# A fixed order on every engine after the first chunk, and value products and the next scores in one burst

## The chip, the cores and the metric

The kernel runs on one core of one Trainium2 chip. The metric is the device time of one execution in microseconds. Three executions of the kernel before took 731.03, 731.56 and 733.35 us; their median is 731.56 us. Lower is better.

## The reference

Attention over 8 batches, 8 heads, 576 tokens and head size 64, with two sparse masks, feeds a gated network that takes the largest of three products:

```python
mask_local = (rel >= 0) & (rel < stride)                 # stride 32, heads 0 to 3
mask_strided = (rel >= 0) & (pos[None, :] % stride == pos[:, None] % stride)   # heads 4 to 7
attn = softmax(where(mask, q @ k.T / 8, -1e9))
x = (attn @ v) as (4608 tokens, 512)
h = np.maximum(np.maximum(x @ w1, x @ w2), x @ w3)       # (4608, 768)
return h @ w_out                                         # (4608, 512)
```

## The kernel before, in words

**Units and chunks.** Attention is cut into 32 units, four for each batch; a unit is two heads. In a batch the two strided units come first, then the two local ones. The network works on nine chunks of 512 tokens, and chunk c can start when the units of batch c are done.

**A unit.** `scores(n)` multiplies queries with keys into the PSUM tile `s_ps` (64 or 36 small matmuls, each run twice by the engine because they are float32: 128 or 72 matmuls in the trace, line 266). VectorE adds the mask, takes the maximum and subtracts it (`less_maximum`, lines 287 to 290), ScalarE takes the exponential (line 294), and VectorE sums, inverts, multiplies and transposes into `pt` (`probabilities`, lines 302 to 307). `values(n)` multiplies `pt` with the values into `o_ps` (line 363: 64 matmuls in a strided unit; line 333: 84 in a local one). `leading` (ScalarE, line 391) and `rest` (VectorE, line 395) split the result into the two float32r parts `xh` and `xl` that the network reads.

**A chunk.** It has 22 pieces. Pieces 0 to 17 are `ff_in`, 12 matmuls of 512 columns each (line 410), with `ff_max` behind (line 421 on ScalarE or 423 on VectorE; every third time also line 426 on ScalarE and 427 on GpSimd). Pieces 18 to 21 are `ff_out`, 18 such matmuls (line 436), with a copy and a store (lines 441, 442). I call these matmuls dense. Their results go to two PSUM buffers `f_ps`, so piece i+2 waits until the result of piece i is read.

**What sets the order.** The opening (all weights, the units of batches 0 and 1, and chunk 0) is written out by hand in `OPENING`; each letter is a step, and `pin` holds it in program order. From batch 2 on, `pinned[0]` is False: a scheduler orders the instructions of all engines after its own estimate. The program there puts `begin(n)` (scores to transpose) ahead of pieces 0, 5, 10 and 15 and `end(n)` (values, leading, rest) ahead of pieces 4, 9, 14 and 19. Chunks 7 and 8 have no units beside them.

Of the kernel before, what the change touches and what calls it, by code (L numbers as in the profile page):

```python
# [15 lines left out]
B, H, S, D = 8, 8, 576, 64  # L16
STRIDE = 32
DM, DF, DO = 512, 768, 512
P = 128
# [12 lines left out]
MB = 5  # L32
MS = STRIDE // 4
PAIRED = 2
CH = 512
NCHUNK = B * S // CH
W_LEAST = 2.0**-15
W_MOST = 122877.984375
NKC = DM // P
NJ = DF // P  # L40
# [8 lines left out]
N5 V4 A10 A11 M3 F4 B9 C9 B10 F5 C10 H4 M4 A12 S6 M5 X6 A13 F6 B11 B12 F7 M6 C11 L4 F8 C12 B13 E6 M7 A14  # L49
C13 V5 A15 A16 F9 M8 B14 C14 B15 A17 B16 M9 C15 B17 A18 C16 A19 F10 M10 F11 C17 B18 F12 C18 M11 H5 M12  # L50
N6 F13 A20 F14 L5 A21 B19 V6 C19 A22 M13 F15 B20 C20 M14 F16 M15 A23 F17 B21 M16 B22 C21 C22 S7 M17 B23
X7 C23 H6 O0 E7 L6 N7 O1 Q0 O2 V7 Q1 H7 L7 O3 Q2 Q3
"""


# [1 line left out]
def fused_kernel(ctx, tc, qT, kT, qk_loc, qk_str, v_loc, v_str, m_loc, m_str, w1, w2, w3, w_out, out):  # L57
# [17 lines left out]
    early_ps = ExitStack()  # L75
    ps_e = early_ps.enter_context(tc.tile_pool(name="ps_e", bufs=1, space=bass.MemoryType.PSUM))

    pinned = [True]

    def pin(ins):  # L80

        return tc.keep_in_program_order(ins) if pinned[0] else ins


    mloc = const.tile([P, MB, TK], F32, name="mloc")
# [104 lines left out]
    units = [(b, p) for b in range(B) for p in (2, 3, 0, 1)]  # L190
    loaded = {}

    def load_qk(n):
        if n >= len(units):
            return
        b, p = units[n]
        t = (io_early if n in (2, 3) else io).tile([P, 2, S], F32, name="qk_t", bufs=2)
        if b < EARLY:
            pin(nc.sync.dma_start(out=t[:, 0, :], in_=qT[b, p]))
            pin(nc.sync.dma_start(out=t[:, 1, :], in_=kT[b, p]))  # L200
        else:
            src = qk_loc[b - EARLY, p, 0] if p < 2 else qk_str[b - EARLY, p - 2].rearrange("p x s -> p (x s)")
            src = src.rearrange("p (x h s) -> p x h s", x=2, h=2)
            for h in range(2):
                hs = slice(h * D, (h + 1) * D)
                pin(nc.sync.dma_start(out=t[hs], in_=src[hs, :, h, :]))
        loaded[n] = [t.rearrange("p x s -> p (x s)")]
# [27 lines left out]
    state = {}  # L235

    def scores(n):


        b, p = units[n]  # L240
        t = loaded[n][0]
        s_ps = s_places[0 if n in (0, 2) else 1]
        mask = mloc.rearrange("p m k -> p (m k)") if p < 2 else mstr.unsqueeze(1).broadcast_to([P, MS, NI])
        first = n < 8
        if first:
            for h in range(2):
                flat = s_ps[:, h, : MB * TK] if p < 2 else s_ps[:, h, : 32 * MS].rearrange("p (m k) -> p m k", m=MS)
                pin(nc.tensor.matmul(flat if p < 2 else flat[:, :, :NI], unit, mask, start=True, stop=False))  # L248
        nm, w, at = (MB, TK, TK) if p < 2 else (MS, NI, 32)
        pairs = p >= 2 and b >= PAIRED  # L250
        for m in range(nm):
            for j in range(4):
                if p < 2:
                    u = j * MB + m
                    if u >= NT:
                        continue

                    q0, k0 = 32 * u, S + 32 * u - 32
                else:

                    q0 = NI * (j * MS + m)
                    k0 = S + q0
                k1 = m * 64 + j % 2 * 32 if pairs else m * at
                for h in range(2):
                    hs = slice(h * D, (h + 1) * D)
                    pin(nc.tensor.matmul(  # L266
                        s_ps[32 * j : 32 * (j + 1), h, k1 : k1 + w],
                        t[hs, q0 : q0 + 32],
                        t[hs, k0 : k0 + w],
                        start=not first,  # L270
                        stop=not first or m == (2 if p < 2 and j == 3 else nm - 1),
                    ))
        if pairs:
            s = s_ps.rearrange("p h (m r k) -> p h m r k", r=2, k=32)[:, :, :, :, :NI]
            flat, mask, axes = s, mpair.unsqueeze(1).unsqueeze(1), AX.XY
            wide = lambda x: x[:, :, :nm].unsqueeze(3).unsqueeze(4).broadcast_to(list(s.shape))
        else:
            s = s_ps[:, :, : nm * at].rearrange("p h (m k) -> p h m k", m=nm)[:, :, :, :w]
            flat, mask, axes = (s_ps[:, :, : nm * w] if p < 2 else s), mask.unsqueeze(1), AX.X
            wide = lambda x: x[:, :, :nm].unsqueeze(3).broadcast_to([P, 2, nm, w])  # L280
        state[n] = s_ps, s, wide, nm, 2 * at if pairs else at, axes, None if first else (flat, mask)

    def less_maximum(n):
        s_ps, s, wide, nm, at, axes, masked = state[n]
        if masked:
            flat, mask = masked
            pin(nc.vector.tensor_tensor(out=flat, in0=flat, in1=mask.broadcast_to(list(flat.shape)), op=ALU.add))  # L287
        mx = att.tile([P, 2, MS], F32, name="mx")
        pin(nc.vector.tensor_reduce(out=mx[:, :, :nm], in_=s, op=ALU.max, axis=axes))
        pin(nc.vector.tensor_tensor(out=s, in0=s, in1=wide(mx), op=ALU.subtract))  # L290

    def exponentials(n):
        s = state[n][1]
        pin(nc.scalar.activation(out=s, in_=s, func=AF.Exp, scale=SCALE))  # L294

    def probabilities(n):

        s_ps, s, wide, nm, at, axes, _ = state[n]
        sm = att.tile([P, 2, MS], F32, name="sm")

        sums = sm[:, :, :nm] if nm * at == 512 else s_ps[:, :, 512 - MS : 512 - MS + nm]
        pin(nc.vector.tensor_reduce(out=sums, in_=s, op=ALU.add, axis=axes))
        pin(nc.vector.tensor_scalar(out=sums, in0=sums, scalar1=EPS, scalar2=None, op0=ALU.add))
        pin(nc.vector.reciprocal(out=sm[:, :, :nm], in_=sums))
        pin(nc.vector.tensor_tensor(out=s, in0=s, in1=wide(sm), op=ALU.mult))
        pt = att.tile([P, 2, 512], F32, name="pt")
        pin(nc.vector.transpose(pt[:, :, : nm * at], s_ps[:, :, : nm * at]))  # L307
        state[n] = pt
# [80 lines left out]
    def leading(n):  # L389
        for src, hi, lo in state[n]:  # L390
            pin(nc.scalar.copy(out=hi, in_=src))  # L391

    def rest(n):
        for src, hi, lo in state.pop(n):
            pin(nc.vector.tensor_tensor(out=lo, in0=src, in1=hi.bitcast(F32), op=ALU.subtract))  # L395
# [4 lines left out]
    def ff_in(c, j, i):  # L400
        if not ps_f:
            early_ps.close()
            ps_f.append(ctx.enter_context(tc.tile_pool(name="ps_f", bufs=2, space=bass.MemoryType.PSUM)))
        f_ps = ps_f[0].tile([P, 512], F32, name="f_ps")
        hi, lo = x_chunk(c)
        wh, wl = weight[i, j]

        for kc in (2, 3, 0, 1):
            for n, (w, x) in enumerate(((wh, hi), (wh, lo), (wl, hi))):
                pin(nc.tensor.matmul(  # L410
                    f_ps, w[:, kc, :], x[:, kc, :], start=(kc == 2 and n == 0), stop=(kc == 1 and n == 2)
                ))
        hs[c, j, i] = f_ps
# [15 lines left out]
    def ff_out(c, t):  # L429
        f_ps = ps_f[0].tile([P, 512], F32, name="f_ps")  # L430
        ts = slice(t * P, (t + 1) * P)
        for j in range(NJ):
            hh, hl = hs[c, j]
            wh, wl = weight[None, j]
            for n, (h, w) in enumerate(((hh, wh), (hl, wh), (hh, wl))):
                pin(nc.tensor.matmul(f_ps, h[:, ts], w, start=(j == 0 and n == 0), stop=(j == NJ - 1 and n == 2)))  # L436
        hs[c, "out", t] = f_ps

# [2 lines left out]
        pin(nc.scalar.copy(out=o_sb, in_=hs.pop((c, "out", t))))  # L441
        pin(nc.scalar.dma_start(out=out[c * CH + t * P : c * CH + (t + 1) * P, :], in_=o_sb))

    def chunk(c):
        def both(do, then, *args):
            do(c, *args)
            then(c, *args)

        pieces = [lambda j=j, i=i: both(ff_in, ff_max, j, i) for j in range(NJ) for i in range(3)]
        return pieces + [lambda t=t: both(ff_out, ff_store, t) for t in range(CH // P)]  # L450


    def begin(n):
        scores(n)
        load_qk(n + 2)
        less_maximum(n)
        exponentials(n)
        probabilities(n)

    def end(n):  # L460
        values(n)
        load_v(n + 2)
        leading(n)
        rest(n)

    load_weights(1, nc.scalar)
    pin(nc.scalar.activation(out=nothing, in_=nothing, func=AF.Exp))
# [5 lines left out]
    for n in (2, 3):  # L473
# [7 lines left out]
    load_v(5)  # L481
    load_weights(len(sources))
    steps = {
        "S": scores, "X": less_maximum, "E": exponentials, "N": probabilities, "V": values, "H": leading, "L": rest,
        "A": lambda n: convert_begin(), "B": lambda n: convert_bits(), "C": lambda n: convert_end(),
        "F": lambda n: ff_in(0, n // 3, n % 3), "M": lambda n: ff_max(0, n // 3, n % 3),
        "O": lambda n: ff_out(0, n), "Q": lambda n: ff_store(0, n),
# [1 line left out]
    for step in OPENING.split():  # L489
# [3 lines left out]
            load_qk(n + 2)  # L493
        if what == "V" and n >= 4:
            load_v(n + 2)
    pinned[0] = False

    for b in range(2, B):
        for i, piece in enumerate(chunk(b - 1)):
            if i % 5 == 0 and i < 20:  # L500
                begin(4 * b + i // 5)
            if i % 5 == 4:
                end(4 * b + i // 5)
            piece()
    for c in range(B - 1, NCHUNK):
        for piece in chunk(c):
            piece()


# [64 lines left out]
```

## Time and profile before

| | |
|---|---|
| median of three executions | 731.56 us |
| the profiled execution | 728.72 us |
| its span, first to last instruction | 727.0 us |
| TensorE busy (PE) | 694.8 us, 96% |
| weight loads (PEld) | 560.2 us, 77% |
| VectorE, ScalarE, GpSimd | 313.8, 171.1, 123.0 us |
| matmuls, weight loads | 8448 and 8448 |
| chain that ended last, TensorE's share | 86% |

Each matmul has one weight load ahead of it, which runs beside the matmul before. The chain that ended last is followed back from the last instruction, so a large share of one engine in it says that this engine's work sets the time. Matmul durations in the rows are longer than their spacing, because each starts while the one before drains; the spacing of the starts is what counts.

### The profile page before, as it was taken

The page shows a single profiled execution, that of the slowest core. Times are in us where ns is not written, and L with a number is a line of the kernel's source. Part 1 is how long each engine was busy: PE and PEld are TensorE (multiplying, and loading weights), DVE is VectorE, ACT ScalarE, POOL GpSimd, SP SyncE. Part 2 cuts the span into 40 slices and gives each one's busy share as a digit, 9 for nine tenths or more (in the row PEclk, how much of TensorE's full clock was granted, in tenths as well). Part 3 has the DMA queues.
Part 4 walks back from the last instruction along what each step waited for, and adds up shares of the span by engine and source line. Part 5 has one row for each costly group of instructions (what it writes and reads, how often), then busy time and mean ns, then how long its engine had stood idle before and what let it go on. Part 6 is the DMA issues. An engine that isn't in the chain of part 4 may idle for free.

```text
span 727.0 us, 18760 instructions
## 1 busy us (share of the span) xinstructions
PE 694.8 (96%) x8448; PEld 560.2 (77%) x8448; DVE 313.8 (43%) x527; ACT 171.1 (24%) x346; POOL 123.0 (17%) x129
## 2 busy tenths in 40 slices
PE   6369899999999999999999999999999999999997
PEld 5258677888788878888788878887888788888886
DVE  6778995445334442545155514552344401101110
ACT  2546663121211221221112211212122211111111
POOL 4337572011001110111001100110001101100110
PEclk9569999999999999999999999999999999999999
DMA  7998011322222123212221222232220010000001
GB/s 242 263 306 305 25 31 63 96 67 71 71 77 55 55 76 107 54 54 62 90 82 58 63 73 62 62 82 73 62 55 22 15 44 1 0 30 29 1 1 58
DMA packets 35808, 55.35 MB, mean 76 GB/s; under 512 B 5200, under 2 KB 18512, under 8 KB 35728
## 3 DMA queue, kind: packets, MB, share of 16 engines
q1 hardware_dynamic: 30016, 44.19, 21.0%
q10 hardware_dynamic: 5712, 9.96, 3.7%
q8 instruction: 66, 1.08, 0.6%
q14 instruction: 14, 0.11, 0.1%
HBM read 44.70 MB, written 9.44 MB: 74 GB/s over the span
## 4 chain that ended last, share of the span: by engine, by line
PE 86%; DVE 1%; ACT 0%; issue 0%; DVEq 0%
PE f_ps L410 57%; PE f_ps L436 21%; PE s_ps L266 4%; PE o_ps L333 2%; PE o_ps L363 2%; ACT work L441 0%; DVE work L163 0%; DVE h_max L423 0%; PE s_ps L248 0%; DVE o_ps L160 0%; DVE work L166 0%; DVEq L166 0%; DVEq L160 0%
## 5 line engine op out<-in xcount | busy, mean ns | idle before, releaser
L410 PE MATMUL f_ps<-xh,w 128*128 128x512 f32 x1296 | 415.3, 395 | 2.7 <-ACT h_max L421 1.9
L410 PEld LDWEIGHTS f_ps<-xh,w 128*128 128x128 f32 x1296 | 243.8, 188 | 56.8 <-ACT h_max L421 2.3
L410 PE MATMUL f_ps<-xl,w 128*128 128x512 f32 x648 | 253.3, 391 | 0.0
L427 POOL TENSOR_TENSOR hl<-h_max,hh 128x512 fp32r<-128x512 f32 x54 | 69.6, 1289 | 532.4 <-ACT hh L426 532.4
L423 DVE TENSOR_TENSOR h_max<-f_ps,h_max 128x512 f32<-128x512 f32 x108 | 74.6, 690 | 187.9 <-PE f_ps L410 187.8
L436 PE MATMUL f_ps<-wNone,hh 128*128 128x512 f32 x432 | 140.6, 396 | 0.4 <-ACT work L441 0.4
L410 PEld LDWEIGHTS f_ps<-xl,w 128*128 128x128 f32 x648 | 122.1, 188 | 24.0
L436 PEld LDWEIGHTS f_ps<-wNone,hh 128*128 128x128 f32 x432 | 81.0, 188 | 18.9 <-ACT work L441 1.3
L436 PE MATMUL f_ps<-wNone,hl 128*128 128x512 f32 x216 | 85.1, 394 | 0.0
L426 ACT CAST hh<-h_max 128x512 fp32r<-128x512 f32 x54 | 33.5, 620 | 200.8 <-DVE h_max L423 200.8
L395 DVE TENSOR_TENSOR xl<-o_ps,xh 128x320 fp32r<-128x320 f32 (+11 forms) x96 | 28.2, 349 | 84.1 <-ACT xh L391 84.1
L266 PEld LDWEIGHTS s_ps<-qk_t 64*32 64x32 f32 x3200 | 34.4, 110 | 22.8 <-issue 20.1
L441 ACT COPY work<-f_ps 128x512 f32<-128x512 f32 x36 | 21.0, 588 | 120.7 <-PE f_ps L436 120.7
L421 ACT COPY h_max<-f_ps 128x512 f32<-128x512 f32 x54 | 31.7, 586 | 74.1 <-PE f_ps L410 42.7
L266 PE MATMUL s_ps<-qk_t 64*32 64x18 f32 (+1 forms) x3200 | 39.6, 206 | 8.8 <-issue 6.3
L436 PEld LDWEIGHTS f_ps<-wNone,hl 128*128 128x128 f32 x216 | 40.6, 188 | 8.2
L294 ACT ACTIVATE s_ps<-s_ps 128x640 f32<-128x640 f32 (+2 forms) x32 | 20.3, 634 | 83.1 <-DVE s_ps L290 82.8
L287 DVE TENSOR_TENSOR s_ps<-s_ps,mpair 128x576 f32<-128x576 f32 x12 | 9.2, 767 | 68.1 <-PE s_ps L266 68.1
L391 ACT CAST xh<-o_ps 128x320 fp32r<-128x320 f32 (+11 forms) x96 | 24.3, 329 | 34.9 <-PE o_ps L333 30.4
L307 DVE STREAM_TRANSPOSE pt<-s_ps 128x640 f32<-128x640 f32 (+2 forms) x32 | 31.4, 980 | 0.7
L333 PEld LDWEIGHTS o_ps<-pt,v_t 32*64 32x64 f32 x1344 | 18.6, 141 | 16.2 <-issue 10.2
L333 PE MATMUL o_ps<-pt,v_t 32*64 32x64 f32 (+1 forms) x1344 | 22.3, 238 | 7.2 <-DVE xl L395 3.3
(49 smaller groups left out, 336.3 us busy)
## 6 DMA issues: line engine op xcount, KB each, us to landing
out<-work ACTq DMA_DIRECT2D x36, 256.0 KB
w<-in_w SPq DMA_DIRECT2D x17, 512.0 KB
qk_t<-in_qT SPq DMA_DIRECT2D x28, 288.0 KB
qk_t<-in_kT SPq DMA_DIRECT2D x28, 288.0 KB
v_t<-in_v_str SPq DMA_DIRECT2D x48, 128.0 KB
v_t<-in_v_loc SPq DMA_DIRECT2D x48, 96.0 KB
wNone<-in_w_out SPq DMA_DIRECT2D x6, 512.0 KB
v_t<-in_v_str SPq DMA_DIRECT2D x16, 72.0 KB
```

Of the source, the lines that this page charges most:

```text
L266: pin(nc.tensor.matmul(s_ps[32 * j : 32 * (j + 1), h, k1 : k1 + w], t[hs, q0 : q0 + 32], t[hs, k0 : k0 + w], start=not first, stop=not fir ...
L307: pin(nc.vector.transpose(pt[:, :, : nm * at], s_ps[:, :, : nm * at]))
L333: pin(nc.tensor.matmul(o[h * D : (h + 1) * D, j, 32 * max(m, 0) : 32 * max(m, 0) + width], v[js, h, m + 1, :], pt[js, h, m * TK + 32 : m * ...
L391: pin(nc.scalar.copy(out=hi, in_=src))
L395: pin(nc.vector.tensor_tensor(out=lo, in0=src, in1=hi.bitcast(F32), op=ALU.subtract))
L410: pin(nc.tensor.matmul(f_ps, w[:, kc, :], x[:, kc, :], start=(kc == 2 and n == 0), stop=(kc == 1 and n == 2)))
L421: pin(nc.scalar.copy(out=a, in_=f_ps))
L423: pin(nc.vector.tensor_tensor(out=a, in0=f_ps, in1=a, op=ALU.max))
L426: pin(nc.scalar.copy(out=hh, in_=a))
L427: pin(nc.gpsimd.tensor_tensor(out=hl, in0=a, in1=hh.bitcast(F32), op=ALU.subtract))
L436: pin(nc.tensor.matmul(f_ps, h[:, ts], w, start=(j == 0 and n == 0), stop=(j == NJ - 1 and n == 2)))
L441: pin(nc.scalar.copy(out=o_sb, in_=hs.pop((c, "out", t))))
```

## The change

From chunk 1 on the scheduler's freedom is gone: `pin` is now always `keep_in_program_order`, and a new loop writes out the order. The value products of unit n stand ahead of pieces 3, 8, 13 and 18 (`BURSTS`), and the scores of unit n+1 directly behind them; then come the split of unit n, the mask and maximum of n+1, the piece itself, the exponential, and one piece later the probabilities, with the transpose split off into `transposed` behind that piece's `ff_max`. The scores of unit 8 move into the opening, behind the values of unit 7. In `ff_out` the low weight part now comes ahead of the low half of h. The number of instructions that compute is the same.

```diff
+BURSTS = (3, 8, 13, 18)
-X7 C23 H6 O0 E7 L6 N7 O1 Q0 O2 V7 Q1 H7 L7 O3 Q2 Q3
+X7 C23 H6 O0 E7 L6 N7 O1 Q0 O2 V7 S8 Q1 H7 L7 O3 Q2 Q3
-    pinned = [True]
-    def pin(ins):
-        return tc.keep_in_program_order(ins) if pinned[0] else ins
+    pin = tc.keep_in_program_order
-            for n, (h, w) in enumerate(((hh, wh), (hl, wh), (hh, wl))):
+            for n, (h, w) in enumerate(((hh, wh), (hh, wl), (hl, wh))):
-    pinned[0] = False
-    for b in range(2, B):
-        for i, piece in enumerate(chunk(b - 1)):
-            if i % 5 == 0 and i < 20:
-                begin(4 * b + i // 5)
-            if i % 5 == 4:
-                end(4 * b + i // 5)
-            piece()
+    for c in range(1, NCHUNK):
+        coming = None
+        if c == 1:
+            coming = 8
+            less_maximum(coming)
+        for i in range(3 * NJ + CH // P):
+            if i in BURSTS and c < B - 1:
+                n = 4 * (c + 1) + BURSTS.index(i)
+                coming = n + 1 if n + 1 < len(units) else None
+                values(n)
+                if coming:
+                    scores(coming)
+                load_v(n + 2)
+                leading(n)
+                rest(n)
+                if coming:
+                    load_qk(coming + 2)
+                    less_maximum(coming)
+                since = i
+            elif i == 0:
+                since = 0
++            if i < 3 * NJ:
+                ff_in(c, i // 3, i % 3)
+            else:
+                ff_out(c, i - 3 * NJ)
+            if coming and i == since:
+                exponentials(coming)
+            if coming and i == since + 1:
+                probabilities(coming)
++            if i < 3 * NJ:
+                ff_max(c, i // 3, i % 3)
+            else:
+                ff_store(c, i - 3 * NJ)
+            if coming and i == since + 1:
+                transposed(coming)
+                coming = None
```

In the rows of the order below, a float32 matmul counts once (the trace shows it twice), and line numbers of after are two higher or lower (363 is 365, 266 is 264, 410 is 412, 436 is 438, 333 is 335, 395 is 397, 423 is 425).

TensorE in chunk 1, around the values of unit 8; `o_ps<-pt,v_t` are values, `s_ps<-qk_t` scores, `f_ps` dense. Before:

```order
L410 MATMUL f_ps<-xh,w_1_805 128x512
L363 MATMUL o_ps<-pt,v_t 64x2x18 x32
L410 MATMUL f_ps<-xh,w_1_815 128x512
L410 MATMUL f_ps<-xl,w_1_815 128x512
L410 MATMUL f_ps<-xh,w_1_815 128x512 x2
L410 MATMUL f_ps<-xl,w_1_815 128x512
L410 MATMUL f_ps<-xh,w_1_815 128x512 x2
L410 MATMUL f_ps<-xl,w_1_815 128x512
L410 MATMUL f_ps<-xh,w_1_815 128x512 x2
L410 MATMUL f_ps<-xl,w_1_815 128x512
L410 MATMUL f_ps<-xh,w_1_815 128x512
L266 MATMUL s_ps<-qk_t 32x18 x64
```

One piece of 12 dense matmuls stands between the values of unit 8 and the scores of unit 9. After:

```order
L412 MATMUL f_ps<-xl,w_0_663 128x512
L412 MATMUL f_ps<-xh,w_0_663 128x512
L365 MATMUL o_ps<-pt,v_t 64x2x18 x32
L264 MATMUL s_ps<-qk_t 32x18 x64
L412 MATMUL f_ps<-xh,w_1_805 128x512
L412 MATMUL f_ps<-xl,w_1_805 128x512
```

The two stand together, and the pieces between such bursts are five.

TensorE at the end of chunk 1, the values of unit 11. Before:

```order
L436 MATMUL f_ps<-wNone_1664,hh 128x512
L333 MATMUL o_ps<-pt,v_t 64x64 x7
L436 MATMUL f_ps<-wNone_1719,hh 128x512
L333 MATMUL o_ps<-pt,v_t 64x64 x4
L436 MATMUL f_ps<-wNone_1719,hl 128x512
L436 MATMUL f_ps<-wNone_1719,hh 128x512
L333 MATMUL o_ps<-pt,v_t 64x64 x3
L333 MATMUL o_ps<-pt,v_t 64x32 x8
L333 MATMUL o_ps<-pt,v_t 64x64 x14
L333 MATMUL o_ps<-pt,v_t 64x32 x6
L436 MATMUL f_ps<-wNone_1485,hh 128x512
```

The scheduler put dense matmuls into the middle of the values, so that they come in three parts. After:

```order
L412 MATMUL f_ps<-xh,w_5_1466 128x512
L335 MATMUL o_ps<-pt,v_t 64x64 x14
L335 MATMUL o_ps<-pt,v_t 64x32 x8
L335 MATMUL o_ps<-pt,v_t 64x64 x14
L335 MATMUL o_ps<-pt,v_t 64x32 x6
L264 MATMUL s_ps<-qk_t 32x18 x64
L438 MATMUL f_ps<-wNone_1485,hh 128x512 x2
```

They are whole, ahead of the first `ff_out`. The scores of units 12, 16, 20, 24 and 28, which before stand in two parts (2 and 62 matmuls), are whole too.

VectorE in chunk 1, from the split of unit 8 on. Before:

```order
L395 TENSOR_TENSOR xl<-o_ps,xh 128x384
L395 TENSOR_TENSOR xl<-o_ps,xh 128x192
L423 TENSOR_TENSOR h_max<-f_ps,h_max 128x512
L287 TENSOR_TENSOR s_ps<-s_ps,mpair 128x32x18
L289 TENSOR_REDUCE mx<-s_ps 128x16
L290 TENSOR_TENSOR s_ps<-s_ps,mx 128x32x18
L423 TENSOR_TENSOR h_max<-f_ps,h_max 128x512
L302 TENSOR_REDUCE sm<-s_ps 128x16
```

After:

```order
L397 TENSOR_TENSOR xl<-o_ps,xh 128x384
L397 TENSOR_TENSOR xl<-o_ps,xh 128x192
L285 TENSOR_TENSOR s_ps<-s_ps,mpair 128x32x18
L287 TENSOR_REDUCE mx<-s_ps 128x16
L288 TENSOR_TENSOR s_ps<-s_ps,mx 128x32x18
L299 TENSOR_REDUCE sm<-s_ps 128x16
L300 TENSOR_SCALAR sm<-sm 128x16
L301 RECIPROCAL sm<-sm 128x16
L302 TENSOR_TENSOR s_ps<-s_ps,sm 128x32x18
L425 TENSOR_TENSOR h_max<-f_ps,h_max 128x512
L309 STREAM_TRANSPOSE pt<-s_ps 128x1024
```

Between the split and the probabilities no `h_max` stands any more, and one now stands ahead of the transpose.

## Rows read from the trace of the kernel before

**Rows 1.** The page: granted TensorE clock in 40 slices (tenths); the queue of instruction packets.
```profile
PEclk9569999999999999999999999999999999999999
...
q8 instruction: 66, 1.08, 0.6%
```

**Rows 2.** Busy time in stretches: PE, PEld, DVE, ACT, POOL, each (xcount); then clock, DMA.
```profile
105.00:727.00 622.00, 617.80 (x6734) 498.59 (x6732) 229.86 (x387) 117.61 (x246) 69.70 (x55) 1.00 0.18 55
```

**Rows 3.** Waits of PE, 130 us to the end: who waited, total us, times, longest.
```profile
PE f_ps L436 <- ACT work L441: 0.4, 2, 0.2
```

**Rows 4.** Timeline of PE around values of unit 8, scores of unit 9: start, us, what.
```profile
141.99 0.39 PE L410 MATMUL f_ps<-xh,w 128*128 128x512 f32 x1
142.30 1.14 PE L363 MATMUL o_ps<-pt,v_t 64*64 64x36 f32 x64
143.37 0.50 PE L410 MATMUL f_ps<-xh,w 128*128 128x512 f32 x1
143.71 0.39 PE L410 MATMUL f_ps<-xl,w 128*128 128x512 f32 x1
143.94 0.63 PE L410 MATMUL f_ps<-xh,w 128*128 128x512 f32 x2
...
146.00 0.39 PE L410 MATMUL f_ps<-xh,w 128*128 128x512 f32 x1
146.32 1.42 PE L266 MATMUL s_ps<-qk_t 64*32 64x18 f32 x128
```

**Rows 5.** Timeline of PE, values of unit 11 at the end of chunk 1.
```profile
191.64 0.36 PE L333 MATMUL o_ps<-pt,v_t 32*64 32x64 f32 x14
...
192.37 0.34 PE L333 MATMUL o_ps<-pt,v_t 32*64 32x64 f32 x8
...
193.31 0.89 PE L333 MATMUL o_ps<-pt,v_t 32*64 32x64 f32 x62
```

**Rows 6.** Timeline of PE, the opening: scores with values directly behind.
```profile
14.27 1.12 PE L266 MATMUL s_ps<-qk_t 64*32 64x64 f32 x72
15.32 1.70 PE L374 MATMUL o_ps<-pt,v_t 18*64 18x18 f32 x128
```

**Rows 7.** Timeline of PEld, the opening: idle time ahead and its releaser in brackets.
```profile
11.14 0.55 PEld L266 LDWEIGHTS s_ps<-qk_t 64*32 64x32 f32 x42 [1.02 <-issue]
...
42.41 0.32 PEld L266 LDWEIGHTS s_ps<-qk_t 64*32 64x32 f32 x29 [4.47 <-issue]
```

**Rows 8.** Busy time in stretches that end where PEld stood still for "issue".
```profile
0.00:11.10 11.10, 5.23 (x222) 4.48 (x222) 4.27 (x10) 3.12 (x5) 7.49 (x28) 1.00 0.83 258
11.10:19.60 8.50, 7.39 (x254) 5.11 (x254) 7.78 (x15) 2.13 (x4) 0.96 (x2) 1.00 0.66 186
19.60:34.50 14.90, 4.15 (x255) 3.68 (x255) 11.89 (x21) 7.18 (x14) 5.26 (x6) 0.57 0.95 298
34.50:42.40 7.90, 3.09 (x127) 2.60 (x128) 3.24 (x7) 2.51 (x6) 1.87 (x2) 0.50 1.10 294
```

**Rows 9.** Busy time in two stretches with the same number of weight loads.
```profile
7.10:11.14 4.04, 3.13 (x160) 2.70 (x149) 2.43 (x7) 0.40 (x1) 1.93 (x8) 1.00 0.96 256
...
296.90:301.40 4.50, 4.50 (x159) 3.68 (x152) 1.51 (x3) 0.94 (x3) 0.00 (x0) 1.00 0.23 59
```

**Rows 10.** Busy time and clock in stretches with idle TensorE.
```profile
18.20:21.50 3.30, 1.31 (x73) 0.89 (x72) 2.44 (x4) 0.97 (x2) 1.89 (x2) 1.00 0.73 208
21.60:25.00 3.40, 0.00 (x0) 0.00 (x0) 1.38 (x2) 1.22 (x3) 0.61 (x1) 0.50 0.73 216
...
84.00:88.00 4.00, 2.15 (x10) 1.49 (x9) 3.66 (x6) 2.15 (x5) 2.54 (x3) 1.00 0.07 16
```

**Rows 11.** Timeline of PEld, dense matmuls while the clock is at half.
```profile
47.04 0.33 PEld L410 LDWEIGHTS f_ps<-xl,w 128*128 128x128 f32 x1
47.47 0.76 PEld L410 LDWEIGHTS f_ps<-xh,w 128*128 128x128 f32 x2
```

**Rows 12.** Timeline of DVE: mask (first) and transpose (last step) of unit 9.
```profile
147.79 0.77 DVE L287 TENSOR_TENSOR s_ps<-s_ps,mpair 128x576 f32<-128x576 f32 x1 [0.61 <-PE s_ps L266]
...
153.44 1.25 DVE L307 STREAM_TRANSPOSE pt<-s_ps 128x1024 f32<-128x1024 f32 x1
```

More of the change, by code (lines that the diff above doesn't have):

```diff
@@ L305, in probabilities, with transposed @@
         pin(nc.vector.tensor_tensor(out=s, in0=s, in1=wide(sm), op=ALU.mult))
+        state[n] = s_ps, nm, at
+    def transposed(n):
+        s_ps, nm, at = state[n]
         pt = att.tile([P, 2, 512], F32, name="pt")
@@ L442, in ff_store @@
         pin(nc.scalar.dma_start(out=out[c * CH + t * P : c * CH + (t + 1) * P, :], in_=o_sb))
[L444 to L464, printed above, removed]
     load_weights(1, nc.scalar)
@@ L483, in fused_kernel @@
     steps = {
-        "S": scores, "X": less_maximum, "E": exponentials, "N": probabilities, "V": values, "H": leading, "L": rest,
+        "S": scores, "X": less_maximum, "E": exponentials, "N": lambda n: (probabilities(n), transposed(n)),
+        "V": values, "H": leading, "L": rest,
         "A": lambda n: convert_begin(), "B": lambda n: convert_bits(), "C": lambda n: convert_end(),
@@ L495, in fused_kernel @@
             load_v(n + 2)
-    pinned[0] = False
-    for b in range(2, B):
-        for i, piece in enumerate(chunk(b - 1)):
-            if i % 5 == 0 and i < 20:
-                begin(4 * b + i // 5)
-            if i % 5 == 4:
-                end(4 * b + i // 5)
-            piece()
-    for c in range(B - 1, NCHUNK):
-        for piece in chunk(c):
-            piece()
+    for c in range(1, NCHUNK):
[19 more added lines that the diff above has]
+                since = 0
+            if i < 3 * NJ:
+                ff_in(c, i // 3, i % 3)
[5 more added lines that the diff above has]
+                probabilities(coming)
+            if i < 3 * NJ:
+                ff_max(c, i // 3, i % 3)
[4 more added lines that the diff above has]
+                coming = None
 _INS = ["qT", "kT", "qk_loc", "qk_str", "v_loc", "v_str", "m_loc", "m_str", "w1", "w2", "w3", "w_out"]
```

## The prediction

> **What bounds the kernel now.** I read the slices of the page first: the clock is low only in the first tenth, at full level from there on [rows 1]. Then the busy time by stretch: from 105 us to the end TensorE works 617.8 of 622.0 us [rows 2], and its waits on other engines there come to 0.4 us [rows 3]. VectorE works 229.9 and ScalarE 117.6 us of the same stretch [rows 2]; what they do is hidden as long as nobody waits. So a time can only change in TensorE's own spacing or by a new wait of TensorE. The opening is left as it was, but for the scores of unit 8.
>
> The spacing is in the timeline [rows 4]. Dense matmuls start every 0.227 us (143.71 to 143.94 is one step). Around a burst of small matmuls this is disturbed: the first small one starts 0.31 us after the last dense one (141.99 to 142.30); the last of the 64 starts about 143.22 (the group ends at 143.44, and one takes 0.22); 0.15 us later comes the first dense one at 143.37, and the next 0.34 us after that. Without a burst two dense steps would stand there, 0.45 us. So each burst pays 0.31 + 0.15 + 0.34 - 0.45 = 0.35 us for being a burst, whatever is in it.
>
> **The change, part by part.**
>
> *Fewer bursts.* Before, values and the next scores are two bursts with 12 dense matmuls between them; after, they are one, 24 times (units 7 and 8 to 30 and 31). Each saves 0.35 us and pays for the seam between the two kinds of small matmul. The trace has one seam, scores with values directly behind: the group of 72 begins at 14.27 and ends at 15.39, its last matmul starts about 15.17, the first value matmul at 15.32 [rows 6], so 0.15. In a group neighbours start about 0.015 apart (0.92 us over 63 steps [rows 4]), and the entry from dense costs 0.31. The seam lies between 0.015 and 0.31; I take 0.13, near the one that I see. 24 x (0.35 - 0.13) = 5.3 us; the bounds give 8.0 and 1.0.
>
> *No split bursts.* The values of units 11, 15, 19, 23, 27 and 31 come in three parts [rows 5], the scores of units 12, 16, 20, 24 and 28 in two. Whole, they save 6 x 2 + 5 = 17 bursts at 0.35, 6.0 us. With 0.4 us [rows 3], which come from two `ff_out` pieces that the scheduler let end together, that makes 6.4. The sum of gains is 5.3 + 6.4 = 11.7, about **12 us** with the small delays of later dense steps after each burst.
>
> *Instructions arrive in packets.* This is what speaks against the change. The page has a queue of 66 instruction packets [rows 1]; 16,896 matmuls and weight loads by 66 are 256 each, 128 pairs. In the opening the weight loads stand still four times for "issue", 1.0 to 4.5 us, the first and the last shown [rows 7]. Counted in loads these stops come after load 222, then 254, 255 and 128 further on [rows 8]: one packet is 128 loads, and a few semaphore instructions make up the missing ones. So TensorE stops at borders of packets, when the next has not come. From load 70 or so to the end of the first stop 149 loads took 4.04 us; elsewhere 152 loads in 4.50 us ran without a stop [rows 9]. I read from it: about 150 loads, one packet and what is read ahead, cannot go by in less than some 4.0 to 4.5 us.
>
> Before, this never bites in the later part: the 12 dense matmuls between values and scores take 2.7 us and give the packet its time. After, 150 loads fit into one burst: some 55 values at 0.0145 and 95 scores at 0.0097 (1.24 us for 128 [rows 4]) with the seam are 1.8 us, of a local unit 1.5; I take 1.7. A burst that holds such a stretch from end to end stops for 4.0 - 1.7 = 2.3 us. Which ones do follows from counting: from the last stop at load 859 every 128 loads (less the semaphores) through the new order of TensorE. The borders lie late in the scores of units 13, 20, 24 and 29, near matmul 99, 88, 123 and 114 of 128, with 150 loads of burst ahead; one lies just behind the scores of unit 17, 3.3 us after the packet was ordered, and stops about 0.7. 4 x 2.3 + 0.7 = **9.9 us**. With 4.5 us in place of 4.0 it is 4 x 2.8 + 1.2 = 12.4, with 3.8 it is 8.9. If the count is shifted against the borders, other bursts stop: over all shifts I count 8.9 to 15.7, mean 12.9.
>
> The Trainium skill says otherwise (Runtime: NRT & Kernel Launch, Instruction fetch mechanics): blocks of 256 instructions, but 2048 of them held for TensorE, and a crossing mostly hidden. Blocks of 256 agree with the 66 packets; 2048 held does not agree with a stop after 222 loads and 222 matmuls [rows 8]. By that page the stops would be 0 and the sum the first rival below.
>
> *The clock.* In the opening a stretch with two idle spells of TensorE (0.89 us of loads in 3.30) was followed by half the granted clock; 4.0 us with 1.49 us of loads, dense ones around the idle spell, kept the full one [rows 10]. A stop of 2.3 us inside 2 us of small matmuls lies between these. At half level dense matmuls start 0.43 us apart [rows 11] instead of 0.227, so 3 us of it (a stretch at half is 3.4 long [rows 10]) lose 3 x 0.47 = 1.4 us. I take one fall among the four long stops, **1.4 us**; none and all are in the rivals.
>
> *The other engines.* In the new order VectorE does the split, the mask and the maximum ahead of the piece's `h_max`. From mask to end of transpose a unit took 6.9 us, pieces between included (147.79 to 154.69 [rows 12]). After, the next values come five pieces, 13.6 us, behind the scores: 5 us and more are spare. The tightest is piece 3, whose first copy (ScalarE, line 421) now waits behind the exponential: some 6.9 us after the burst began, needed at 7.9 (values, scores, two pieces). So it costs nothing; without that microsecond TensorE would wait once a chunk, six times. The loads on SP's queue keep their place behind the burst that frees their buffer, two units ahead. The order in `ff_out` gives GpSimd 0.23 us more for the last low half, which nobody waits for [rows 3].
>
> **The sum.** -12.0 + 9.9 + 1.4 = -0.7 us. The profiled execution took 728.72 us, so 728.0; against the median of 731.56, which lies 2.8 above that execution, 730.9 us. About 0.3%, 2.2 us, is what a measurement of this kernel can tell from no change; the forecast is the same.
>
> **The rivals.**
>
> 1. *No stops.* If the stops of the opening belong to its start or its busy DMA, all 12 us remain: 719.6. For it: the DMA share there is 0.66 to 1.10 [rows 8] against 0.18 later [rows 2]. Against it: the even distance of the stops. 10%.
> 2. *Stops, but a cheap seam and a clock that holds:* seam 0.02 saves 2.6 more, no fall: -12.0 - 2.6 + 9.9 = -4.7, so 726.9. For it: weight loads of 32 columns may go in beside the last values. 23%.
> 3. *Other borders.* If my count is off, 13 to 15.7 us of stops: -12.0 + 13 (or 15.7) + 1.4 = +2.4 to +5.1, so 734 to 736.7. 10%.
> 4. *The clock falls at every stop.* Slower: five falls cost 7.0, -12.0 + 9.9 + 7.0 = +4.9, so 736.5. The place is the dense matmuls behind the scores of units 13, 17, 20, 24 and 29. It decides from the third fall on (-2.1 + 3 x 1.4 = +2.1). For it: the half clock after the idle spells of the opening [rows 10]. Against it: the values ahead of each stop keep TensorE busy. 15%.
> 5. *`f_ps` late at piece 3*, six waits of up to 1 us: +5 at most, 736. 2%.
>
> **How the numbers follow.** The forecast has 40%. Faster by over 0.3%: rivals 1 and 2 and the edge of the forecast, 0.35. Within: the rest of the forecast and the edge of rival 3, 0.40. Slower: rivals 3, 4 and 5, 0.25. The range holds the forecast, rival 2 with a seam still shorter stops could add to, and rivals 3 to 5 up to their far ends: 725.5 to 737.0. Left out are rival 1 and falls of the clock on top of other borders, some 2 in 10.
>
> **What would show it.** Right: in the profile after, TensorE or its loads idle for "issue" around 2.3 us late in the scores of units 13, 20, 24 and 29, about 25 bursts less than before, dense starts 0.227 apart elsewhere, and the clock at 1.00 but for a slice or two. Rival 1 shows no idle time over 0.4 us behind 105 us; rival 4 shows slices of 0.5 clock behind each stop; rival 5 shows TensorE waiting for line 423's counterpart on ScalarE. The forecast is wrong if the packets of instructions are not what stopped the opening, or if a seam costs as much as a fresh entry.

## The result and the profile after

The change makes the kernel slower by a third of a per cent: 732.65 us (median of 20 executions, 729.98 to 737.31) against 729.79 us for the kernel before in the same comparison (20 executions, 728.45 to 733.64). The ratio is 1.0034, with a 95% interval of 1.0018 to 1.0050; that is 1.3 to 3.6 us, 2.5 in the middle. The time lies inside the range of the prediction, but not in the forecast: "the same" was expected, by a gain of 0.7 us, and a small loss came. The mechanism comes nearest to rival 4: the clock fell behind four of the stops.

The profiled execution of after took 737.31 us, the longest of the 20, so its span says little by itself. The page of after, its span, busy times and granted clock in 40 slices (tenths), against [rows 1]:

```profile
span 735.6 us, 18767 instructions
...
PE 693.7 (94%) x8448; PEld 569.4 (77%) x8448; DVE 312.9 (43%) x527; ACT 171.3 (23%) x346; POOL 122.3 (17%) x129
...
PEclk9559999999999999999999999999999999999999
```

PE works 1.1 us less than before, 693.7 against 694.8, and yet the span is 8.6 us longer. Most of that is in the opening. I cut both traces at the first value product of unit 7, the last step ahead of the edit (124.57 us before, 130.77 after). Stretches of before and then of after: length, then busy us of PE, PEld, DVE, ACT and POOL with counts, granted clock, DMA share, GB/s.

```profile
0.00:124.50 124.50, 96.49 (x1866) 76.82 (x1866) 97.65 (x161) 60.03 (x114) 61.20 (x81) 0.89 0.59 180
124.57:727.00 602.43, 598.23 (x6583) 483.33 (x6582) 216.13 (x366) 111.11 (x232) 61.78 (x48) 1.00 0.18 55
```

```profile
0.00:130.70 130.70, 100.91 (x1866) 80.27 (x1866) 98.14 (x161) 60.25 (x114) 60.62 (x81) 0.86 0.55 172
130.77:735.60 604.83, 592.74 (x6583) 489.14 (x6582) 214.74 (x366) 111.01 (x232) 61.67 (x48) 0.99 0.18 54
```

The opening holds the same 1866 matmuls in both, and takes 6.2 us longer in this one execution of after, with a lower clock (0.86 against 0.89). It varies from execution to execution: in the nine experiments, eight of them with the same opening up to there, the values of unit 7 begin some 125 to 130 us into the span. So I compare kernels by the stretch from there to the end: 602.43 us before, 604.83 after, **+2.4 us**, which agrees with the medians. In that stretch PE is busy 5.5 us less, and idle 12.1 us (604.83 - 592.74) against 4.2. The idle time has one name. Waits of PEld from 130 us on, before and then after: who waited for what, us in total, times, longest.

```profile
PEld s_ps L266 <- issue: 9.5, 27, 0.4
PEld o_ps L333 <- issue: 7.9, 24, 0.4
PEld o_ps L363 <- issue: 4.2, 12, 0.4
```

```profile
PEld s_ps L264 <- issue: 8.6, 5, 2.3
PEld o_ps L335 <- issue: 4.6, 13, 0.4
PEld o_ps L365 <- issue: 4.2, 12, 0.4
PEld f_ps L412 <- issue: 0.7, 1, 0.7
```

Three things are to be seen. The many pauses of 0.4 us or less are entries from dense matmuls into small ones: 63 before, 25 after, so the bursts are merged and whole. Waits on another engine are gone (before had two on ScalarE). And there are five pauses of up to 2.3 us in the scores and one of 0.7 in the dense, which no row of before shows behind the opening.

**A merged burst.** Timeline of PE in after, values of unit 10 with scores of unit 11 behind them (start, us, what), against [rows 4]:

```profile
162.84 0.39 PE L412 MATMUL f_ps<-xh,w 128*128 128x512 f32 x1
163.16 1.14 PE L365 MATMUL o_ps<-pt,v_t 64*64 64x36 f32 x64
164.23 0.97 PE L264 MATMUL s_ps<-qk_t 64*32 64x64 f32 x72
165.13 0.50 PE L412 MATMUL f_ps<-xh,w 128*128 128x512 f32 x1
165.47 0.40 PE L412 MATMUL f_ps<-xl,w 128*128 128x512 f32 x1
```

The entry (162.84 to 163.16) and the two steps at the end are those of before. The last value matmul starts about 164.08, 0.22 us ahead of the group's end at 164.30, and the first score at 164.23: the seam is 0.15, and over the 24 merged bursts it is 0.147 (behind values of a local unit) or 0.153 (behind those of a strided one).

**The stops.** Timeline of PEld in after, units 9, 13, the dense behind 17, units 20, 24 and 29; in brackets the idle time ahead and what ended it:

```profile
146.69 0.63 PEld L264 LDWEIGHTS s_ps<-qk_t 64*32 64x32 f32 x64
148.68 0.63 PEld L264 LDWEIGHTS s_ps<-qk_t 64*32 64x32 f32 x64 [1.35 <-issue]
...
222.96 0.93 PEld L264 LDWEIGHTS s_ps<-qk_t 64*32 64x32 f32 x100
225.50 0.24 PEld L264 LDWEIGHTS s_ps<-qk_t 64*32 64x32 f32 x28 [1.61 <-issue]
...
304.40 0.19 PEld L412 LDWEIGHTS f_ps<-xl,w 128*128 128x128 f32 x1 [0.66 <-issue]
...
349.37 0.83 PEld L264 LDWEIGHTS s_ps<-qk_t 64*32 64x32 f32 x88
352.52 0.48 PEld L264 LDWEIGHTS s_ps<-qk_t 64*32 64x32 f32 x40 [2.31 <-issue]
...
428.13 1.27 PEld L264 LDWEIGHTS s_ps<-qk_t 64*32 64x32 f32 x124
431.13 0.14 PEld L264 LDWEIGHTS s_ps<-qk_t 64*32 64x32 f32 x4 [1.73 <-issue]
...
533.65 1.05 PEld L264 LDWEIGHTS s_ps<-qk_t 64*32 64x32 f32 x115
536.27 0.17 PEld L264 LDWEIGHTS s_ps<-qk_t 64*32 64x32 f32 x13 [1.57 <-issue]
```

The loads stand still behind load 100, 88, 124 and 115 of 128 in units 13, 20, 24 and 29, within one of the places that the counting gave, and once behind unit 17. The stop of unit 9, in the middle of its 128 loads, was not foreseen. As the distance from one start of a matmul to the next, less an ordinary step, the six cost 1.42 (unit 9), 1.70, 0.39, 2.38, 1.81 and 1.64 us, 9.3 together.

What the loads wait for can be read as well, because the trace records when each instruction packet of queue q8 was carried. The stretch of the stop of unit 20 (350.10 to 352.52 in after) holds one packet (count, MB, share of 16 engines):

```profile
q8 instruction: 1, 0.02, 2.3%
```

It was carried from 350.18 to 351.06, so it started when the loads already stood still, and they went on at 352.52, 1.46 us after it had landed. The packets of the other five stops landed at 147.33, 223.94, 302.92, 429.79 and 534.84, each 1.34 to 1.56 us before the loads went on; at the four stops in the opening of before the same distance is 1.45 to 1.54 us.

**The clock.** Stretches of after (columns as above) just behind the stops of units 13, 20 and 29, and the one that follows on the first of them; the one behind unit 24, from 431.3, reads like them:

```profile
226.50:229.90 3.40, 3.40 (x9) 2.62 (x9) 2.54 (x4) 0.64 (x1) 0.00 (x0) 0.50 0.42 109
230.00:233.40 3.40, 3.40 (x16) 2.80 (x15) 1.27 (x4) 0.59 (x1) 0.00 (x0) 1.00 0.21 78
352.80:356.10 3.30, 3.30 (x29) 2.68 (x15) 2.29 (x3) 0.50 (x1) 0.00 (x0) 0.50 0.59 157
...
537.10:540.50 3.40, 3.40 (x10) 2.62 (x9) 2.57 (x4) 0.64 (x1) 0.00 (x0) 0.50 0.58 129
```

Each time the granted clock is 0.50 for some 3.4 us, that is 1.2 GHz instead of 2.4, while TensorE works without a pause; in the first of the stretches 9 dense matmuls pass where the next one takes 16. Dense starts are 0.43 apart there instead of 0.227. Each fall loses 1.4 to 1.5 us, the four of them about 5.9. In tenths of 40 slices, as the page has them, none of this can be seen.

So +2.4 = 9.3 (stops) + 5.9 (clock) - the gain, and the gain, as what is left over, is 12.8 us.

### The profile page after: what moved, and what is told of

Its sections match the earlier page's. It is cut to its first block, busy times and chain, and to the rows that moved or that the text cites. A ratio compares the mean times of both kernels' runs of the same rounds, so it can differ in the third digit from the quotient of the medians.

```text
span 735.6 us, 18767 instructions
## 1 busy us (share of the span) xinstructions
PE 693.7 (94%) x8448; PEld 569.4 (77%) x8448; DVE 312.9 (43%) x527; ACT 171.3 (23%) x346; POOL 122.3 (17%) x129
## 4 chain that ended last, share of the span: by engine, by line
PE 88%; SPq 3%; issue 3%; DVE 2%; DMA 2%; POOL 1%; ACT 1%; DVEq 0%; ACTq 0%; POOLq 0%
PE f_ps L412 59%; PE f_ps L438 20%; PE s_ps L264 4%; PE o_ps L335 2%; PE o_ps L365 2%; DMA qk_t<-in_kT 1%; DVE work L164 1%; SPq L228 1%; SPq L220 1%; DVE o_ps L158 1%; DVE work L161 1%; DMA w<-in_w 1%; SPq L132 1%; POOL wNone L173 0%; POOL w L173 0%
## 5 line engine op out<-in xcount | busy, mean ns | idle before, releaser
L412 PEld LDWEIGHTS f_ps<-xh,w 128*128 128x128 f32 x1296 | 247.2, 191 | 56.8 <-ACT h_max L423 2.3
L412 PEld LDWEIGHTS f_ps<-xl,w 128*128 128x128 f32 x648 | 123.9, 191 | 26.0 <-issue 0.7
L438 PE MATMUL f_ps<-wNone,hh 128*128 128x512 f32 x432 | 136.6, 398 | 0.2 <-POOL wNone L173 0.2
L287 DVE TENSOR_REDUCE mx<-s_ps 128x10 f32<-128x640 f32 (+2 forms) x32 | 24.1, 753 | 11.9 <-PE s_ps L264 11.1
L173 POOL TENSOR_TENSOR w<-work,w 128x512 fp32r<-128x512 f32 x18 | 23.4, 1301 | 31.7 <-ACT w L172 31.7
```

What stands on the lines that cost most here:

```text
L412: pin(nc.tensor.matmul(f_ps, w[:, kc, :], x[:, kc, :], start=(kc == 2 and n == 0), stop=(kc == 1 and n == 2)))
```

## The experiments

For each: the edit, what was expected, what came. "From unit 7" is the stretch from the first value product of unit 7 to the end in the profiled execution, 602.43 us before and 604.83 after.

**1. Every pair apart.** In after, the scores of each unit from 9 on go one piece behind the values, with their loads and their mask; the values stay whole and the order fixed.

```diff
+APART = tuple(range(9, 32))
-                if coming:
+                late = coming in APART
+                if coming and not late:
                     scores(coming)
+            elif late and i == since + 1:
+                late, since = False, i
+                scores(coming)
+                load_qk(coming + 2)
+                less_maximum(coming)
```

> The changed kernel, but the scores of every unit from 9 on stand one piece of 12 dense matmuls behind the values instead of directly behind them. Theory (packets of 256 instructions; a merged burst uses one up faster than the next can come; the stop brings the clock down): no idle time for issue over 0.4 us behind the opening, clock at 1.00 from there on, and of the gains only the whole bursts remain, about -7 us against the kernel before, some 722.5 us. Rival (the stops belong to the fixed order or to late waits, not to the length of the burst): stops of 1.5 us and more stay in the scores of units 13, 20, 24 and 29 and the time stays within 0.5% of the changed kernel.

Measured: 724.41 us (722.63 to 727.31), ratio 0.9915 (0.9884 to 0.9946); from unit 7 595.79. The long stops are gone, and the clock is 1.00 throughout behind the opening. One short stop was not expected, in the scores of unit 12 (PEld of this kernel):

```profile
196.00 0.10 PEld L265 LDWEIGHTS s_ps<-qk_t 64*32 64x32 f32 x1 [0.74 <-issue]
```

It follows that the long stops need the two kinds of small matmul standing together. Against before this kernel gains 6.6 us, or 7.4 without that stop. One merge is left in it (units 7 and 8, some 0.2 us); the rest, 6.4 to 7.2, is the price of the split bursts (foreseen: 6.4, with the 0.4 of waits).

**2. Six pairs apart.** As before, with `APART = (9, 13, 17, 20, 24, 29)`: only the bursts that stopped are taken apart, 18 stay merged.

> The changed kernel, with the scores of units 9, 13, 17, 20, 24 and 29 alone one piece behind the values; the other 18 merged bursts stay. By the count of instructions no border of a packet falls late in a burst that is still merged. Theory: no stops behind the opening but perhaps 0.5 us in the scores of unit 25, clock 1.00, and the gain of the merges comes on top: about -11 us against the kernel before, 718.5 us. Rival (any merged burst may stop): stops of 1.5 us and more turn up in other merged bursts, and the time is 722 to 728 us.

Measured: 720.40 us (718.32 to 721.25), ratio 0.9852 (0.9830 to 0.9875); from unit 7 591.28. Stretch of this kernel from there to near the end, and the waits of PEld in it:

```profile
128.18:717.00 588.82, 587.54 (x6583) 484.28 (x6582) 214.29 (x366) 111.08 (x232) 61.84 (x48) 1.00 0.18 55
```

```profile
PEld o_ps L336 <- issue: 4.6, 13, 0.4
PEld o_ps L366 <- issue: 4.2, 12, 0.4
PEld s_ps L265 <- issue: 2.1, 6, 0.4
```

No pause is over 0.4 us, the clock is 1.00, and PE is idle 1.3 us in 588.8. Giving up 6 of 24 merges wins 13.6 us back (604.83 - 591.28). The stops and falls read in after, 15.2 us, less six merges at 0.22, make 13.9; so the two readings hold. Of the 18 merges that stay experiment 1 has one too; the other 17 are worth 595.79 - 591.28 = 4.5 us, 3.7 without the short stop of experiment 1, that is 0.22 to 0.27 us each (0.35 - 0.13 = 0.22 in the sum).

**3. Instructions shifted by half a packet.** 128 small instructions stand ahead of the opening of after; nothing else differs.

```diff
+    for _ in range(32):
+        pin(nc.tensor.matmul(o[:32, 3, :NI], unit[:64, :32], mstr[:64], start=True, stop=True))
     for step in OPENING.split():
```

> The changed kernel with 32 small float32 products (128 instructions, half a packet) put ahead of the opening; nothing reads what they write. Theory: the stops move to where the borders are now, the scores of units 8, 12, 16, 21 and 28 and the first dense matmul behind the scores of unit 9, 1.3 to 2 us each, and none of the scores of units 13, 20, 24 and 29 stops; six stops and their falls of the clock, 733 to 740 us. Rival (the stops belong to these units, through their loads or waits): units 13, 20, 24 and 29 stop again.

Measured: 737.40 us (736.58 to 739.92), ratio 1.0095 (1.0064 to 1.0126); from unit 7 608.34. Stops of PEld in this kernel, in the scores of units 8, 12, 16 and 28; two like them lie in the dense behind unit 9 (2.15 us idle) and in the scores of unit 21 (2.03), and one short one (0.93 from start to start) behind unit 14:

```profile
132.40 0.15 PEld L264 LDWEIGHTS s_ps<-qk_t 64*32 64x32 f32 x8 [2.43 <-issue]
...
198.89 0.58 PEld L264 LDWEIGHTS s_ps<-qk_t 64*32 64x32 f32 x47 [2.03 <-issue]
...
278.15 0.21 PEld L264 LDWEIGHTS s_ps<-qk_t 64*32 64x32 f32 x11 [1.80 <-issue]
...
509.62 0.34 PEld L264 LDWEIGHTS s_ps<-qk_t 64*32 64x32 f32 x32 [2.09 <-issue]
```

Units 13, 20, 24 and 29 run without a stop; other units have them, the ones that the counting gave. Nothing in units 8 to 31 was edited, only the number of instructions ahead of them. So the place of a stop is set by counting instructions, not by what a unit computes. The rival, that the stops belong to certain data or DMAs, is out. The clock falls three times here, behind units 12, 16 and 28 (behind 16 for 6.8 us, twice as long as in after), and stays at 1.00 behind 8, 9 and 21.

**4. The transpose earlier.** In after, `transposed` stands directly behind `probabilities`, ahead of the piece's `h_max`. This is meant for the stop of unit 9.

```diff
             if coming and i == since + 1:
                 probabilities(coming)
+                transposed(coming)
-                transposed(coming)
                 coming = None
```

> The changed kernel with the transpose directly behind the probabilities, ahead of the maximum of that piece, as one step again. Theory (reading ahead halts at the wait of the values of unit 8, which the transpose answered only 0.5 us before its turn, so that the packet behind was ordered late): the wait is answered some 2 us earlier and the stop of 1.35 us in the scores of unit 9 is gone; the four long stops stay where they are, within a few matmuls; about -1.3 us. Rival: the stop in unit 9 has another cause and stays.

Measured: 730.45 us in one execution; from unit 7 603.47, 1.36 less than after. PEld of this kernel, values of unit 8 and scores of unit 9 (the first row is the values):

```profile
140.18 0.85 PEld L365 LDWEIGHTS o_ps<-pt,v_t 64*64 64x64 f32 x52
141.08 1.29 PEld L264 LDWEIGHTS s_ps<-qk_t 64*32 64x32 f32 x128
```

The 128 loads go through in one run, where after stopped behind 64 of them; the other four long stops stay. The 1.36 us are not the price of that stop alone, and that they come near the 1.3 expected is chance: the clock does not fall behind unit 13, it stays at 0.50 for 6.8 us behind unit 20, and the four stops have other lengths (1.3 to 2.3 us). In after, the timeline of DVE shows what differed ahead of those values, which began at 145.62:

```profile
143.09 0.69 DVE L425 TENSOR_TENSOR h_max<-f_ps,h_max 128x512 f32<-128x512 f32 x1 [1.78 <-PE f_ps L412]
143.69 1.24 DVE L309 STREAM_TRANSPOSE pt<-s_ps 128x1024 f32<-128x1024 f32 x1
```

The transpose stood behind an `h_max` that first waited 1.78 us for TensorE, and ended at 144.93, 0.7 us ahead of the values' turn. The packet for these scores started at 146.19 in after, 0.56 us behind the first value; here it started 1.36 us ahead of it. So the packet came late in after, and that is the stop. My reading was that TensorE's queue does not fetch on past a wait that is not answered. It is not shown, and experiment 6 speaks against it: with the transpose in its old place the packet started 2.4 us before the transpose had ended, and the stop was gone.

**5. Bursts by themselves.** The kernel of experiment 2, and in chunks 7 and 8, which have no units beside them, four small matmuls ahead of each of the 36 `ff_in` pieces.

```diff
+            if c >= B - 1 and i < 3 * NJ:
+                for h in range(2):
+                    pin(nc.tensor.matmul(o[:32, h, :NI], unit[:64, :32], mstr[:64], start=True, stop=True))
```

> The kernel with six units apart, and in chunks 7 and 8, where nothing stands beside the network, two small float32 products (four matmuls in the trace) ahead of each of the 36 ff_in pieces; nothing reads what they write. It measures what a burst costs for being a burst. Theory: 0.35 us each and some 0.03 for the four matmuls, +13 to +14 us against that kernel, 733 to 734 us. Rival (the price lies in what the bursts hold, not in the change between small and dense): only the matmuls themselves, 36 x 0.05, +2 us, 722 us.

Measured: 740.10 us in one execution; from unit 7 608.16 against 591.28, 16.9 us or 0.47 for each. Timeline of PE in this kernel:

```profile
640.90 0.39 PE L413 MATMUL f_ps<-xh,w 128*128 128x512 f32 x1
641.22 0.30 PE L512 MATMUL o_ps<-mstr,unit 64*32 64x18 f32 x4
641.44 0.50 PE L413 MATMUL f_ps<-xh,w 128*128 128x512 f32 x1
641.78 0.40 PE L413 MATMUL f_ps<-xl,w 128*128 128x512 f32 x1
```

The entry is 0.32 and the second dense step 0.34, as around a real burst; four matmuls that do nearly no work cost 0.88 - 0.45 = 0.43 us in this place. A burst's price does not come from its work. The 0.47 is over the expected 0.38; what the rest comes from I did not separate.

**6. Half a piece between.** For units 13, 20, 24 and 29, the piece's first 6 (in `ff_out` 9) dense matmuls go between values and scores.

```diff
+HALVED = (13, 20, 24, 29)
                 values(n)
+                if coming in HALVED:
+                    ff_in(c, i // 3, i % 3, 0) if i < 3 * NJ else ff_out(c, i - 3 * NJ, 0)
                 if coming:
                     scores(coming)
```

> The changed kernel, but for units 13, 20, 24 and 29 half of the piece's dense matmuls (6, or 9 in ff_out; 1.4 or 2 us) stand between the values and the scores. Theory (the packet needs 3.3 to 4 us from its order): the four long stops shrink to 0.2 to 1 us each and the clock stays at 1.00 behind the opening; the stop in the scores of unit 9 stays; 721 to 723 us. Rival (a stop is not made up for by time but by the number of small matmuls in a row): the stops keep 1.5 us and more, and the time stays above 728 us.

Measured: 719.15 us (718.35 to 722.61), ratio 0.9845 (0.9828 to 0.9863); from unit 7 591.41. The waits of PEld behind 130 us:

```profile
PEld s_ps L265 <- issue: 1.7, 5, 0.4
PEld f_ps L413 <- issue: 0.6, 1, 0.6
```

Six dense matmuls, 1.4 us (units 13 and 29), or nine, 2 us (units 20 and 24), are enough to take away stops of 1.6 to 2.4 us and with them all falls of the clock. The stop of unit 9, expected to stay, did not appear. Up to there the order is that of after, and the transpose ended 0.69 us ahead of the values in both; but the packet started 3.11 us ahead of the first value here and 0.56 us behind it in after. Why, I can't tell.

**7. The fixed order alone.** In the kernel before, the scheduler is bound to the order in which its loop is written.

```diff
-    pinned[0] = False
+    pinned[0] = True
```

> The kernel before with its own loop, but held in program order to the end: a fixed order alone, without the new places of the steps. The bursts are whole (-6 to -7 us). VectorE then does all steps of a unit, 6.4 us with the exponential between, ahead of the maximum of the piece behind. Theory: the result of that piece is read too late for the two PSUM buffers, and TensorE waits some 1.8 us behind the scores of two units of each batch (pieces 5 and 10), 12 times: about +21 - 7 = +14 us, 744 us. Rival (the slack of two buffers covers it): 723 us.

Measured: 744.96 us in one execution; from unit 7 616.17, 13.7 more than before. Waits of PE behind 130 us:

```profile
PE f_ps L410 <- DVE h_max L423: 17.8, 12, 1.7
```

Twelve times, twice a chunk, TensorE waits for an `h_max` that stands behind a unit's whole VectorE work. A fixed order is thus no gain by itself; in the order that after writes out, with that work spread over two pieces, no such row appears.

**8. The old order in `ff_out`.** After, with the low half of h ahead of the low weights again.

```diff
-            for n, (h, w) in enumerate(((hh, wh), (hh, wl), (hl, wh))):
+            for n, (h, w) in enumerate(((hh, wh), (hl, wh), (hh, wl))):
```

> The changed kernel with the three products of ff_out in their old order. Theory: the low half of h comes in time either way, so no wait of TensorE on GpSimd and no difference beyond 0.3% to the changed kernel. Rival: TensorE waits for the last low half at the head of ff_out in chunks 7 and 8, up to 0.5 us each.

Measured: 734.01 us (731.53 to 736.56), ratio 1.0058 (1.0027 to 1.0088), which overlaps after's; from unit 7 605.53 against 604.83. The same stops, four falls, no wait on GpSimd. This edit costs and gains nothing that can be told.

**9. Experiments 4 and 6 together.**

> The kernel with half a piece in the bursts of units 13, 20, 24 and 29, and the transpose directly behind the probabilities. Theory: the stop in the scores of unit 9 (1.4 us) goes too; stops of 0.2 to 0.6 us at most are left behind the opening, the clock stays at 1.00, and from the values of unit 7 to the end it takes 590 us against 591.4 of the kernel with the half pieces alone; 718 us, 1.6 to 1.7% below the kernel before. Rival (the earlier transpose delays the maximum of its piece, so that TensorE waits for a PSUM buffer): waits of TensorE on VectorE, 720 us and more.

Measured: 719.40 us (718.08 to 721.92), ratio 0.9850 (0.9824 to 0.9876); from unit 7 592.47, so no better than experiment 6. No stop is left, but a wait of PEld that after does not have:

```profile
PEld f_ps L413 <- DVE h_max L426: 1.2, 2, 0.7
```

With the transpose ahead, the `h_max` behind it comes later by the transpose's 1.24 us, and twice the next piece waits for that. Experiments 2, 6 and 9, about 1.5% below before, beat both kernels.

## Why the prediction came out as it did

**The step that failed is the clock.** "I take one fall among the four long stops, 1.4 us": there were four falls, 5.9 us. That is +4.5 on the sum of -0.7. The size of one fall was right (1.4 to 1.5 us against 1.4), but by luck: the 3.4 us in it were the length of the stretch that I had chosen for [rows 10], and the clock of before reads 0.50 from 21.6 to 48.8 us; only the kernel after showed falls of 3.4 us. The number was not right. [Rows 10] had one row with a fall and one without, and I put the case between them because values ahead of a stop keep TensorE busy. Rival 4 named the place and said that the third fall decides; with four of its five the time came to that side, for which I had 15%. Behind unit 17 and unit 9 the clock held.

**The stops were right, in part by luck.** 9.9 us foreseen, 9.3 measured, and the units and the places in them to within one load. But the four long ones are 1.6 to 2.4 us where I took 2.3 for each, because the time for 150 loads was taken as 4.0 us: with 1.6 to 1.7 us of running loads ahead of a stop it is 3.3 to 4.1. The four together are 7.5 instead of 9.2, and the one behind unit 17 is 0.39 instead of 0.7. Of the missing 2.0 us 1.4 are made up by unit 9, which I had not foreseen. By the rule of 150 loads no stop was due there, since they took 6.9 us (140.32 to 147.22); but the packet started only 0.56 us behind the first value, and the 128 loads from there on ran for 1.6 us. In all six stops of after, this one too, 3.0 to 3.8 us passed from the load 128 places ahead to the first load behind the stop. On the other engines "it costs nothing" holds for waits, none is in the trace; whether the later transpose is what delayed this packet stays open (experiments 4 and 6).

**The gain was right.** 12.0 us foreseen, 12.8 left over in after; experiment 2 by itself gives 11.2 with 18 merges, 12.5 to 12.8 with the other six. Experiment 1 measures the split bursts at 6.4 to 7.2 us (6.4 foreseen), experiments 1 and 2 a merge at 0.22 to 0.27 us (0.22). The seam measured 0.15, not 0.13; the trace of before had shown just that in [rows 6], and I took a little less without a reason from a row. "About 25 bursts less" among the signs does not follow from the sum, which has 24 + 17 = 41; the rows have 63 and 25.

**The page of the Trainium skill** (Runtime: NRT & Kernel Launch, Instruction fetch mechanics) would have left the full 12 us, with crossings mostly hidden. Stops behind the opening at counted places, which move by a half packet with the count (experiment 3) and end 1.2 to 1.6 us after a packet has landed, speak against that for this kernel, as [rows 8] did; the measurement decides.

**The other rivals.** Rivals 1 and 3 are out: the stops are there, and the count was right. So are rival 2, since the seam is 0.15 and the clock fell, and rival 5, since nobody waits for line 423 behind 130 us.

**What was weighted wrongly.** "Same" had 40% and rested on one fall. The sum with none, one, two, three or four falls is -2.1, -0.7, +0.7, +2.1, +3.5; no row ahead told between them, and the chance for "slower" should have been higher than 0.25.

## What to carry to other kernels

Count instructions, not only microseconds: where the weight loads pause for "issue" in an opening, find the count between the pauses and look where it falls in an order that one means to write. Merging bursts of small matmuls removes a fixed price for each (0.2 us here after the seam), but a burst that holds more instructions than arrive in its time stops, and a stop of about 2 us can cost another 1.5 through the clock; a few dense matmuls left between, only where a border falls, keep the merge elsewhere (experiments 2 and 6). Before fixing an order, see which waits the scheduler's freedom had avoided (experiment 7).

## What the runs showed that I had not expected

- **Short stops are enough for the clock.** Pauses of the loads of 1.57, 1.61, 1.73 and 2.31 us in after were each followed by 3.4 us at 0.50. Pauses as long need not be: behind the 2.43 us in unit 8 of experiment 3 the clock stays at 1.00, behind the 2.03 us in unit 21 too (stretch below), and in experiment 4 the stop of unit 13 (1.35 from start to start) had no fall behind it, where after's (1.71) had one. In experiment 7 TensorE waits twelve times for up to 1.7 us between dense matmuls, and its clock reads 1.00 from 130 us to the end. So the length of the pause alone does not decide; what tells these apart stays open. Stretch of experiment 3 behind that stop, columns as above:

```profile
385.00:388.40 3.40, 3.40 (x36) 2.82 (x32) 2.29 (x3) 0.65 (x2) 0.00 (x0) 1.00 0.56 153
```

- **The same order can stop or not.** In after and experiment 8 the packet for the scores of unit 9 started 0.5 to 0.6 us behind the first value, and they stopped for 1.4 us; in experiment 6, with the same order up to there, it started 3.11 us ahead, and nothing stopped. With the transpose earlier (experiments 4 and 9) it started 1.3 to 1.4 us ahead. What sets that start stays open.
- **The opening varies by some 5 us** between executions of the same instructions, some 125 to 130 us to the values of unit 7 in the experiments. A difference of a few us between single profiled executions must be read behind it.
